# A new order of steps at the head of a fused attention and expert kernel, and two routing steps one product sooner

## The chip, the cores and the metric

The kernel runs on one core of a Trainium2 chip. The metric is the time of one execution on the device in microseconds (us), lower is better; the time of a kernel is the median of its runs.

## The reference

The first half is a cross-attention between tokens and a small recurrent state; its output feeds a mixture of experts, in which each token goes to one expert, or to that of the token before it where a gate says so.

```python
# x: 8 x 8 heads x 512 tokens x 64;  state: 8 x 8 x 32 x 64
scores = x @ state.T / 8;  a = softmax(scores);   xread = a @ state      # 512 rows for each batch
scores2 = state @ x.T / 8; a2 = softmax(scores2); sread = a2 @ x         # 32 rows for each batch
x = concat([xread, sread]) with the heads side by side                   # 8 x 576 tokens x 512
logits = x @ w_gate;  local_gate = sigmoid(x @ w_local)
for b, s:                              # in order, since an expert can be the one before
    e = argmax(logits[b, s]) if s == 0 or local_gate[b, s] < 0.5 else the expert of token s - 1
    out[b, s] = softmax(logits[b, s])[e] * (relu(x[b, s] @ w1[e]) @ w2[e])
```

w1 has 8 x 512 x 1024 and w2 8 x 1024 x 512 numbers, all float32.

## The kernel before, in words

Each of the 8 batches is a *unit* of 512 tokens that are all put through one expert (that of the batch's first token); what doesn't fit is done later in small tiles. A unit's two matrix products are made by a scheme with seven products of half size in place of eight, which needs sums and differences of quarters of its operands: `first_sum` (four of w1's quarters), `column_sum` (four of the tokens' quarters), `second_sum` (of w2's). They are made on VectorE (DVE). A unit has four halves with seven products each, 28 in all; `seven` (line 985) writes their order: 1, 5, 6, 2, 7, 3, 4 in the first matrix product. Two PSUM banks take turns with a third, `sum`; product 5 of the next half can only begin when DVE has read product 3 of the half before out of its bank.

All instructions are written out in Python order, and each engine runs its own in that order; an engine waits when the next instruction's operand isn't ready. The order comes from tables. `HEAD` (line 140) is a list of steps that stand ahead of the first product of unit 0: attention for batches 0 and 1. A step is two letters and its batch (and half): `sc` scores on TensorE (PE), `tr` 32x32 transposes on DVE, `mx`, `mo` maxima, `sb` subtraction on GpSimd (POOL), `ex`, `et` exponentials on ScalarE (ACT), `zh`, `zs`, `zi` sums of the exponentials and their inverses, `ml` their shares (POOL), `tb` transposing back (DVE, tile a), `tu` and `ec` transposes on PE and their copy by ACT, `sr`, `st`, `rt` the state's reads, their scaling (ACT) and transpose (DVE, tile rt), `sl`, `lg` logits of state and token rows (PE), `lt` their transpose, `fe` the expert of the first token (five small DVE instructions, and for batch 0 the load of that expert's weights on the SP queue), `vv` the tokens' reads (PE), `xr`, `xd` their copies by ACT or DVE, `ga`, `gl` products of the gate's weights and their copy, `kp n` n matmuls on zeros.

`BESIDE` gives what batch 1 still has to do after that, each name behind the number of a *tick*: a tick is one product of the experts, counted from 1, and its steps are written behind that product. `FLOW` does the same for batches 2 to 7, with 14 ticks for a batch. `GROUPS` gives ticks for the seven parts of `Routing.choose`, which works out each token's expert for batches 0 and 1, 2 and 3, and 4 to 7: part 1 compares logits on DVE, part 2 is an exponential, part 3 transposes on PE (line 585), part 4 is the scan over tokens on DVE (lines 590 and 591), part 5 transposes back on PE (line 601).

In unit 0 the sums of the tokens' and weights' quarters were written where `run` begins (two each, behind HEAD) and at tick 2 (the other two each).

Of the kernel before, what the change touches and what calls it, by code (L numbers as in the profile page):

```python
# [116 lines left out]
class Slots:  # L117


    def __init__(self, pool):  # L120
# [17 lines left out]


HEAD = """  # L140
sc0 tr01 tr00 kp3 ga mo01 mo00 sb01 sc1 gl mx00 sb00 mx01 ex01 tr10 nb0 ex00 zh01 tr11 et00 zh00 zs01 mo10 et01 kp7
tu00 zs00 sb10 zi01 zi00 tu01 mo11 ec00 ml01 mx11 ex10 ec01 mx10 ml00 tb01 kp2 sr0 sb11 iv0 tb00 st0 nb1 kp1 lg0 zh10
ex11 rt0 vv0 lt0 et11 zh11 zs10 fe0 xr02 xd03 et10 sl0 zs11 tu11 xd01 xr00 zi10 zi11 tu10 sk0 ml10 ec11 iv1 ec10
ml11 tb10 kp2 sr1 tb11
"""


BESIDE = """
1 lg1 vv1 st1 / 2 xr10 xr11 lt1 / 3 rt1 fe1 sl1 / 4 xr12 xr13 sk1 / 6 wr12 wr13 / 7 wr10 wr11 / 8 ws0 / 10 ws1 /
11 wr00 wr01 / 12 wr02 wr03  # L150
"""


# [4 lines left out]
"""  # L158
FIRST, PERIOD = 2, 14
PER = 28  # L160
GROUPS = {(0, 2): (6, 9, 9, 11, 13, 14, 15), (2, 4): (57, 60, 61, 62, 64, 65, 67),
          (4, 8): (103, 105, 106, 107, 110, 111, 112)}
ONES = 18, 19, 21, 22, 24, 25, 27, 28, 29

# [1 line left out]
class Attention:  # L166
# [74 lines left out]
    def do(self, name, *at):  # L241
        steps = dict(xt=self.load_t, xn=self.load_n, sc=self.scores, mx=self.maximum, nb=self.scaled, tr=self.turned,
                     zh=self.halves, mo=self.over_states, sb=self.subtract, ex=self.exponents, zs=self.sums,
                     zi=self.inverses, ml=self.shares, tb=self.turn_back, et=self.exponents_over_tokens, tu=self.turn,
                     ec=self.turned_to, iv=self.invert, sr=self.state_reads, st=self.states_to, rt=self.states_turned,
                     ws=self.states_to_rows, sl=self.state_logits, sk=self.state_logits_kept, lg=self.logits,
                     lt=self.logits_turned, vv=self.token_reads, xr=self.reads_kept, xd=self.reads_kept_too,
                     wr=self.reads_out, ga=self.gates, gl=self.gates_kept, kp=self.keep, fe=self.first_expert)
        steps[name](*at)

    def flow(self, at):

        for part in BESIDE.split("/"):
            tick, *names = part.split()
            for name in names:
                at(int(tick), self.named, name)
        for part in FLOW.split("/"):
            tick, *names = part.split()
            for b in range(2, B):
                for name in names:  # L260
                    at(max(3, FIRST + PERIOD * (b - 2) + int(tick)), self.named, name, b)
        for b in range(3, B):
            for h in range(2):
                at(FIRST + PERIOD * (b - 3) + 1, self.load_t, b, h)
            at(FIRST + PERIOD * (b - 3) + 16, self.load_n, b)
        return FIRST + PERIOD * (B - 3) + 32
# [204 lines left out]
class Routing:  # L471
# [82 lines left out]
    def choose(self, bank, b0, b1):  # L554
# [34 lines left out]
        hold, run = self.hold[:n], self.ran[:n]  # L589
        nc.vector.tensor_scalar(hold, seq, 0.0, None, Alu.is_equal)  # L590
        nc.vector.tensor_tensor_scan(run, hold, seq, 0.0, Alu.mult, Alu.add)
        zp = flat(self.zp)
        nc.vector.tensor_reduce(zp, pr, axis=AX, op=Alu.add)
# [210 lines left out]
class Experts:  # L804
# [72 lines left out]
    def at(self, tick, do, *args):  # L877
        self.todo.setdefault(tick, []).append(lambda: do(*args))

    def tick(self):  # L880
        self.ticks += 1
        for do in self.todo.pop(self.ticks, ()):
            do()
# [5 lines left out]
    def run(self, start):  # L889
# [13 lines left out]
        h11, h21, c12, h22 = [fh.tile([P, FK // 2, UNIT // 2], F32, name=f"h{i}") for i in range(4)]  # L903
        h1 = ctx.enter_context(tc.tile_pool(name="h1", bufs=1))
        ending = ExitStack()
        for i in range(2):
            self.column_sum(i)
            self.first_sum(i)

        tile_at = {}  # L910

# [260 lines left out]
        at = self.at  # L1172
# [4 lines left out]
                    at(PER * u + 18 + i, self.column_sum, i)  # L1177
                    at(PER * u + 22 + i, self.first_sum, i)
        start.flow(at)
        for do, i in ((self.column_sum, 2), (self.first_sum, 2), (self.first_sum, 3), (self.column_sum, 3)):  # L1180
            at(2, do, i)
        at(2, start.zero_row)
        for (b0, b1), ticks in GROUPS.items():
            self.steps(route.choose(start.bank, b0, b1), *ticks)
        tick = max(max(t) for t in GROUPS.values()) + 1
        at(tick, tiles_begin)
# [100 lines left out]
```

## Time and profile before

| | |
|---|---|
| median of 3 runs | 503.4 us (502.07, 504.11, 503.40) |
| the profiled execution | 505.37 us, of which the trace's span is 503.6 us |
| PE busy | 486.3 us, 97% of the span |
| DVE busy | 271.3 us, 54% |
| ACT busy | 161.2 us, 32% |
| POOL busy | 73.8 us, 15% |
| chain that ended last | PE 90%, DVE 3%, DMA 3% |
| mean granted clock of PE | 0.991 of 2.4 GHz |

An engine's busy time is the union of its instructions' spans. A row of the timeline gives an instruction's start, its length and, in brackets, how long the engine stood idle before it and what ended that. The span leaves out 1.8 us of the execution that lie around it.

### The profile page before, as it was taken

The numbers are of one execution on the slowest core, as the hardware profiler recorded it, in microseconds if no ns is written. First come the engines' busy times: TensorE is split into PE (matmuls) and PEld (weight loads), VectorE is DVE, ScalarE is ACT, GpSimd is POOL, SyncE is SP. The second block draws the span as 40 slices with busy tenths as digits, with TensorE's granted clock in tenths as the row PEclk, the third lists the DMA queues.
The fourth block names the chain that finished last, engine by engine and source line by source line (L and its number), as shares of the span: only waits on it lengthen the run. The fifth ranks groups of instructions, "written<-read, shape, count | busy, mean of one in ns | idle before, by whom it ended". The sixth has DMA issues, their size and how long they took to land.

```text
span 503.6 us, 9993 instructions
## 1 busy us (share of the span) xinstructions
PE 486.3 (97%) x4008; PEld 392.2 (78%) x4008; DVE 271.3 (54%) x540; ACT 161.2 (32%) x334; POOL 73.8 (15%) x100
## 2 busy tenths in 40 slices
PE   8779999999999899999999999999999999999994
PEld 2447788787878678888888888888888888888883
DVE  5867885585955858436475945155241632535211
ACT  2524325345343353434222322222123221223210
POOL 6601132212221122200000020000101000000000
PEclk9998999999999899999999999999999999999999
DMA  8966382845929148261717986693998659694411
GB/s 313 343 268 224 130 328 68 271 174 182 367 105 313 49 162 306 89 211 42 286 49 255 402 320 215 241 381 123 401 378 323 241 210 405 229 352 163 169 50 48
DMA packets 40479, 115.66 MB, mean 230 GB/s; under 512 B 7764, under 2 KB 8152, under 8 KB 36200
## 3 DMA queue, kind: packets, MB, share of 16 engines
q1 hardware_dynamic: 39704, 113.76, 61.7%
q0 software_dynamic: 576, 1.12, 0.6%
q8 instruction: 33, 0.54, 0.4%
q14 instruction: 22, 0.18, 0.1%
q10 hardware_dynamic: 144, 0.07, 0.0%
HBM read 97.10 MB, written 17.89 MB: 228 GB/s over the span
## 4 chain that ended last, share of the span: by engine, by line
PE 90%; DVE 3%; DMA 3%; POOL 1%; SPq 1%; issue 1%; ACT 0%; DVEq 0%; POOLq 0%
PE ps L1102 23%; PE ps L1056 21%; PE sum L1102 16%; PE sum L1056 16%; PE ps L972 3%; PE ps L959 3%; PE s L320 2%; DMA a<-in_w_dram 1%; DMA x_t<-in_xt_dram 1%; PE p L390 1%; PE p L403 1%; PE s L449 1%; DVE a L848 1%; PE p L435 1%; POOL e L380 0%
## 5 line engine op out<-in xcount | busy, mean ns | idle before, releaser
L1056 PE MATMUL ps<-x,a 128*128 128x256 f32 x384 | 92.9, 385 | 1.5 <-DMA a<-in_w_dram 1.5
L1056 PE MATMUL sum<-xs,a 128*128 128x256 f32 x384 | 92.8, 385 | 0.0
L1056 PEld LDWEIGHTS ps<-x,a 128*128 128x128 f32 x384 | 72.2, 192 | 17.2 <-issue 5.8
L1056 PEld LDWEIGHTS sum<-xs,a 128*128 128x128 f32 x384 | 73.4, 193 | 10.9 <-issue 0.6
L1102 PE MATMUL ps<-c,h 128*128 128x256 f32 x264 | 63.4, 383 | 0.0
L1102 PE MATMUL ps<-c,hs 128*128 128x256 f32 x256 | 60.7, 380 | 0.0
L1102 PE MATMUL sum<-c,h 128*128 128x256 f32 x248 | 58.6, 379 | 0.0
L1102 PEld LDWEIGHTS ps<-c,h 128*128 128x128 f32 x264 | 49.1, 190 | 11.1 <-issue 5.0
L1102 PEld LDWEIGHTS ps<-c,hs 128*128 128x128 f32 x256 | 48.5, 190 | 6.6
L1102 PEld LDWEIGHTS sum<-c,h 128*128 128x128 f32 x248 | 47.1, 190 | 6.4
L848 DVE TENSOR_TENSOR a<-a,a 128x1024 f32<-128x1024 f32 x32 | 39.6, 1275 | 5.5 <-DMA a<-in_w_dram 5.3
L848 DVE TENSOR_TENSOR c<-c,c 128x1024 f32<-128x1024 f32 x32 | 38.9, 1249 | 1.8 <-DMA c<-in_w_dram 1.5
L848 DVE TENSOR_TENSOR h<-s,s 128x512 f32<-128x512 f32 x16 | 11.1, 692 | 52.2 <-ACT s L1085 52.1
L992 ACT COPY sum<-ps 128x512 f32<-128x512 f32 (+1 forms) x32 | 14.8, 464 | 55.9 <-PE ps L1056 29.0
L1056 PE MATMUL ps<-xs,a 128*128 128x256 f32 x128 | 30.9, 384 | 1.2 <-DVE a L848 1.2
L1085 ACT COPY s<-sum 128x512 f32<-128x512 f32 x32 | 18.8, 586 | 39.4 <-PE sum L1056 39.1
L848 DVE TENSOR_TENSOR xs<-x 128x512 f32<-128x512 f32 x16 | 10.9, 679 | 38.1 <-DMA x<-xts 38.1
L1102 PE MATMUL sum<-c,hs 128*128 128x256 f32 x128 | 30.7, 382 | 0.0
L924 POOL DMA_INDIRECT xgt<-rows,state x9 | 10.0, 1111 | 139.7 <-DMA ct<-in_w_dram 74.7
L1106 ACT ACTIVATE s<-sum,prob 128x256 f32<-128x256 f32 x32 | 15.2, 474 | 43.6 <-PE sum L1102 43.6
L1056 PEld LDWEIGHTS ps<-xs,a 128*128 128x128 f32 x128 | 24.3, 191 | 5.3 <-DVE a L848 2.1
L848 DVE TENSOR_TENSOR y<-s,s 128x256 f32<-128x256 f32 x16 | 6.7, 421 | 37.9 <-ACT s L1106 37.8
(187 smaller groups left out, 560.3 us busy)
## 6 DMA issues: line engine op xcount, KB each, us to landing
at<-in_w_dram SPq DMA_DIRECT2D x18, 1024.0 KB, 6.7
ct<-in_w_dram SPq DMA_DIRECT2D x18, 1024.0 KB, 8.0
a<-in_w_dram SPq DMA_DIRECT2D x32, 512.0 KB, 7.4
c<-in_w_dram SPq DMA_DIRECT2D x32, 512.0 KB, 9.1
x_t<-in_xt_dram SPq DMA_DIRECT2D x16, 512.0 KB, 4.6
x_n<-in_xn_dram SPq DMA_DIRECT2D x8, 1024.0 KB, 12.2
out_dram<-y SPq DMA_DIRECT2D x31, 256.0 KB, 4.1
xts<-xr SPq DMA_DIRECT2D x28, 256.0 KB, 2.6
```

Source lines behind the costliest of these rows:

```text
L320: self.nc.tensor.matmul(s[u][32 * k:32 * k + 32, :], lhsT=self.states(b)[r, k, :], rhs=self.get(f"x_t{k // 2}", b)[r, k % 2, :], start=Tru ...
L390: self.nc.tensor.transpose(t[:, q], self.get("e2", b, u)[:, q], self.route.ident)
L403: self.nc.tensor.matmul(r[32 * k:32 * k + 32, u, :], lhsT=e[:, c, u, 32 * k:32 * k + 32], rhs=x_n[:, c, u, k, :], start=(c == 0), stop=(c ...
L848: self.nc.vector.tensor_tensor(out, a, b, op=op)
L924: nc.gpsimd.indirect_dma_start(out=to.rearrange("p k x -> p (k x)"), out_offset=None, in_=rows.rearrange("n q x -> (n q) x"), in_offset=ba ...
L959: nc.tensor.matmul(hps[SQ * g:SQ * g + SQ, :], lhsT=self.x_t[:, j, :], rhs=a[:, j, :, g], start=(j == 0), stop=(j == KT - 1))
L972: nc.tensor.matmul(yps[SQ * g:SQ * g + SQ, :], lhsT=self.h[:, m, :], rhs=self.ct[:, 2 * m // FK, g // 2, m % (FK // 2), g % 2 * P:g % 2 * ...
L992: nc.scalar.copy(y, x)
L1056: nc.tensor.matmul(to[:, m * width:m * width + width], lhsT=w[:, j, f:f + P], rhs=x[:, j, :], start=begin and m == 0 and j == 0, stop=(m = ...
L1085: return lambda t: nc.scalar.copy(to, t)
L1102: nc.tensor.matmul(to, lhsT=x[:, m, n * P:n * P + P], rhs=w[:, m, :], start=begin and m == 0, stop=(m == FK // 2 - 1), skip_group_check=True)
L1106: return lambda t: nc.scalar.activation(to, t, Act.Copy, scale=p)
```

## The change

The tables HEAD and BESIDE get another order, the four column sums and four weight sums of unit 0 become steps with names (`cs`, `fs`) that stand in these tables, as does the write of a zero row (`ze`), and in GROUPS three numbers are one lower: parts 1 and 2 for batches 0 and 1 (6 to 5, 9 to 8) and part 4, the scan, for batches 2 and 3 (62 to 61). FLOW's steps for batch 2 begin at tick 4 in place of 3. No instruction is added or removed.

```diff
 HEAD = """
-sc0 tr01 tr00 kp3 ga mo01 mo00 sb01 sc1 gl mx00 sb00 mx01 ex01 tr10 nb0 ex00 zh01 tr11 et00 zh00 zs01 mo10 et01 kp7
...
+sc0 kp1 tr01 kp2 tr00 mo01 sc1 mo00 sb01 mx01 kp3 sb00 mx11 ex01 kp7 tr11 zh01 ex00 mx00 ga zs01 zh00 mx10 nb0 zi01
...
 BESIDE = """
-1 lg1 vv1 st1 / 2 xr10 xr11 lt1 / 3 rt1 fe1 sl1 / 4 xr12 xr13 sk1 / 6 wr12 wr13 / 7 wr10 wr11 / 8 ws0 / 10 ws1 /
...
+1 lg1 lt1 cs3 fe1 fs3 fs2 xr12 / 2 ze / 3 xr11 / 4 sl1 sk1 / 6 wr12 wr13 / 7 wr10 wr11 / 8 ws0 / 10 ws1 / 11 wr00 wr01 /
...
-GROUPS = {(0, 2): (6, 9, 9, 11, 13, 14, 15), (2, 4): (57, 60, 61, 62, 64, 65, 67),
+GROUPS = {(0, 2): (5, 8, 9, 11, 13, 14, 15), (2, 4): (57, 60, 61, 61, 64, 65, 67),
           (4, 8): (103, 105, 106, 107, 110, 111, 112)}
...
-                at(max(3, FIRST + PERIOD * (b - 2) + int(tick)), self.named, name, b)
+                at(max(4, FIRST + PERIOD * (b - 2) + int(tick)), self.named, name, b)
...
-        for i in range(2):
-            self.column_sum(i)
-            self.first_sum(i)
...
-        for do, i in ((self.column_sum, 2), (self.first_sum, 2), (self.first_sum, 3), (self.column_sum, 3)):
-            at(2, do, i)
-        at(2, start.zero_row)
```

Three places show what moves. The first is DVE about the first sums of unit 0; a_92 to a_95 are the weights' quarters, a_96 to a_98 their sums (a_94 is written over by the third), xs the tokens' sums, and rt batch 1's transposed state reads. Before:

```order
L384 STREAM_TRANSPOSE a<-e_372 128x512
L848 TENSOR_TENSOR xs_88<-x 128x512
L848 TENSOR_TENSOR a_96<-a_94,a_95 128x1024
L848 TENSOR_TENSOR xs_89<-x,xs_88 128x512
L848 TENSOR_TENSOR a_97<-a_96,a_92 128x1024
L439 STREAM_TRANSPOSE lt<-p 128x128
L848 TENSOR_TENSOR xs_90<-x 128x512
L848 TENSOR_TENSOR a_94<-a_92,a_94 128x1024
L848 TENSOR_TENSOR a_98<-a_93,a_97 128x1024
L848 TENSOR_TENSOR xs_91<-x,xs_89 128x512
L413 STREAM_TRANSPOSE rt<-ys 128x128
```

And now:

```order
L385 STREAM_TRANSPOSE a<-e_392 128x512
L849 TENSOR_TENSOR xs_90<-x 128x512
L414 STREAM_TRANSPOSE rt<-ys 128x128
L849 TENSOR_TENSOR xs_89<-x,xs_88 128x512
L849 TENSOR_TENSOR a_96<-a_94,a_95 128x1024
L849 TENSOR_TENSOR a_97<-a_96,a_92 128x1024
L440 STREAM_TRANSPOSE lt<-p 128x128
L849 TENSOR_TENSOR xs_91<-x,xs_89 128x512
```

The transpose of rt and three of the four token sums now stand ahead of the first sum of weights; behind these rows come the five small instructions of the first expert and then a_98 and a_94.

The second is PE in the same stretch; a product on x or xs and a is one of the experts' products, L423 and L424 are the state's logits of batch 1, L320 and L321 the scores of batch 2, L449 and L450 the token reads of batch 1, of which the last of 16 matmuls stands here. Before:

```order
L449 MATMUL p<-a,states_of 32x512 x2
L1056 MATMUL ps<-xs_88,a_96 128x256 x4
L1056 MATMUL sum<-xs_89,a_97 128x256 x4
L423 MATMUL p<-wgs,rt 32x9 x4
L320 MATMUL s<-x_t_161,sttc_143 32x512 x4
L320 MATMUL s<-x_t_163,sttc_143 32x512 x4
L1056 MATMUL ps<-x,a_93 128x256 x4
L1056 MATMUL sum<-xs_90,a_94 128x256 x4
```

And now:

```order
L450 MATMUL p<-a,states_of 32x512 x2
L1054 MATMUL ps<-x,a_92 128x256 x4
L436 MATMUL p<-a,gl 32x128 x8
L1054 MATMUL ps<-xs_88,a_96 128x256 x4
L1054 MATMUL sum<-xs_89,a_97 128x256 x4
L1054 MATMUL ps<-x,a_93 128x256 x4
L424 MATMUL p<-wgs,rt 32x9 x4
L321 MATMUL s<-x_t_161,sttc_143 32x512 x4
L321 MATMUL s<-x_t_163,sttc_143 32x512 x4
L1054 MATMUL sum<-xs_90,a_94 128x256 x4
```

The token reads have moved from behind product 1 (on a_92) to ahead of it, and product 2 (on a_93) from behind the state's logits and the scores to ahead of them.

The third is DVE in unit 2, at the scan for batches 2 and 3; h and hs are the hidden rows of a half and their sums, of which the second h reads product 3 out of its bank. Before:

```order
L848 TENSOR_TENSOR hs_613<-hs_612,h_615 128x512
L1079 SCALAR_TENSOR_TENSOR h_617<-h_617,h_615 128x512
L350 TENSOR_REDUCE m_1635<-e_1748 128x16
L590 TENSOR_SCALAR hold<-p 2x544
L591 SCALAR_TENSOR_TENSOR ran<-hold,p 2x544
L593 TENSOR_REDUCE zp<-pr 128x10
L594 TENSOR_SCALAR zp<-zp 128x10
L595 RECIPROCAL zp<-zp 128x10
L848 TENSOR_TENSOR hs_614<-h_616,hs_613 128x512
```

And now:

```order
L591 TENSOR_SCALAR hold<-p 2x544
L592 SCALAR_TENSOR_TENSOR ran<-hold,p 2x544
L594 TENSOR_REDUCE zp<-pr 128x10
L595 TENSOR_SCALAR zp<-zp 128x10
L596 RECIPROCAL zp<-zp 128x10
L849 TENSOR_TENSOR h_652<-s_1655,s_1653 128x512
L849 TENSOR_TENSOR h_651<-ps,s_1654 128x512
L1075 SCALAR_TENSOR_TENSOR hs_646<-h_651,h_652 128x512
L849 TENSOR_TENSOR hs_647<-hs_646,h_649 128x512
```

The scan (named SCALAR_TENSOR_TENSOR here, line 592) and what goes with it stand ahead of the half's sums in place of behind them. In unit 0, part 1 of the routing for batches 0 and 1 (lines 571 to 577) has moved in the same way, from behind the five sums of the first half to ahead of them.

## Rows read from the trace of the kernel before

**Rows 1.** The page: the span.
```profile
span 503.6 us, 9993 instructions
```
**Rows 2.** Waits of PE: engine line <- what ended it: us in total, times, longest.
```profile
PE p L423 <- DVE first L546: 2.0, 1, 2.0
PE p L601 <- DVE ran L591: 1.7, 1, 1.7
```
**Rows 3.** Timeline of PE, 24 to 45 us: start, length, line, tiles, [idle before].
```profile
25.25 1.99 PE L1056 MATMUL ps<-x,a 128*128 128x256 f32 x8 [1.50 <-DMA a<-in_w_dram]
27.17 0.64 PE L435 MATMUL p<-a,gl 128*32 128x128 f32 x16
...
30.70 1.99 PE L1056 MATMUL ps<-xs,a 128*128 128x256 f32 x8 [1.17 <-DVE a L848]
32.53 1.90 PE L1056 MATMUL sum<-xs,a 128*128 128x256 f32 x8
36.42 0.39 PE L423 MATMUL p<-wgs,rt 128*32 128x9 f32 x8 [1.99 <-DVE first L546]
36.74 1.87 PE L320 MATMUL s<-x_t,sttc 64*32 64x512 f32 x16
38.54 2.86 PE L1056 MATMUL ps<-x,a 128*128 128x256 f32 x8
41.24 1.89 PE L1056 MATMUL sum<-xs,a 128*128 128x256 f32 x8
```
**Rows 4.** Windows: length, busy of PE, PEld, DVE, ACT, POOL, then granted clock, DMA.
```profile
37.00:40.00 3.00, 3.00 (x20) 1.19 (x5) 1.35 (x5) 0.00 (x0) 0.00 (x0) 0.50 0.11 35
...
170.00:173.00 3.00, 3.00 (x9) 2.38 (x8) 2.93 (x7) 0.59 (x1) 0.00 (x0) 0.51 0.00 0
```
**Rows 5.** Timeline of DVE, 19 to 38 us.
```profile
19.08 0.44 DVE L371 TENSOR_REDUCE z<-zh 128x16 f32<-128x272 f32 x1
...
20.16 0.14 DVE L552 CAST first<-first 1x1 int32<-1x1 f32 x1
...
24.23 0.71 DVE L384 STREAM_TRANSPOSE a<-e 128x512 f32<-128x512 f32 x1 [0.29 <-POOL e L380]
...
29.42 1.23 DVE L848 TENSOR_TENSOR a<-a,a 128x1024 f32<-128x1024 f32 x1 [3.90 <-DMA a<-in_w_dram]
...
33.10 2.35 DVE L848 TENSOR_TENSOR a<-a,a 128x1024 f32<-128x1024 f32 x2
...
35.96 0.31 DVE L413 STREAM_TRANSPOSE rt<-ys 128x128 f32<-128x128 f32 x1
```
**Rows 6.** Timeline of PE, 57 to 66 us: the scores of batch 3.
```profile
60.81 1.09 PE L320 MATMUL s<-x_t,sttc 64*32 64x512 f32 x16
```
**Rows 7.** Timeline of PE, 156 to 176 us.
```profile
167.99 0.25 PE L601 MATMUL p<-identb,ran 2*128 2x2 bf16 x4 [1.70 <-DVE ran L591]
...
168.58 2.40 PE L1056 MATMUL ps<-xs,a 128*128 128x256 f32 x8
170.78 3.21 PE L1056 MATMUL sum<-xs,a 128*128 128x256 f32 x8
```
**Rows 8.** Timeline of DVE, 156 to 176 us.
```profile
161.16 0.69 DVE L848 TENSOR_TENSOR h<-s,s 128x512 f32<-128x512 f32 x1 [2.86 <-ACT s L1085]
...
166.21 0.42 DVE L590 TENSOR_SCALAR hold<-p 2x544 bf16<-2x544 bf16 x1
...
168.44 0.63 DVE L848 TENSOR_TENSOR hs<-h,hs 128x512 f32<-128x512 f32 x1
```
**Rows 9.** Timeline of DVE, 42 to 66 us.
```profile
43.78 0.69 DVE L848 TENSOR_TENSOR h<-s,s 128x512 f32<-128x512 f32 x1 [1.96 <-ACT s L1085]
...
48.49 1.03 DVE L572 TENSOR_TENSOR eq<-lt,mx 128x80 f32<-128x80 f32 x1
...
50.35 0.68 DVE L848 TENSOR_TENSOR hs<-h,hs 128x512 f32<-128x512 f32 x1
```
**Rows 10.** Timeline of POOL, 42 to 66 us.
```profile
48.38 1.05 POOL L357 TENSOR_TENSOR e<-e,m 128x512 f32<-128x512 f32 x1 [5.43 <-DVE m L350]
```

More of the change, by code (lines that the diff above doesn't have):

```diff
@@ L140 @@
 HEAD = """
-sc0 tr01 tr00 kp3 ga mo01 mo00 sb01 sc1 gl mx00 sb00 mx01 ex01 tr10 nb0 ex00 zh01 tr11 et00 zh00 zs01 mo10 et01 kp7
-tu00 zs00 sb10 zi01 zi00 tu01 mo11 ec00 ml01 mx11 ex10 ec01 mx10 ml00 tb01 kp2 sr0 sb11 iv0 tb00 st0 nb1 kp1 lg0 zh10
-ex11 rt0 vv0 lt0 et11 zh11 zs10 fe0 xr02 xd03 et10 sl0 zs11 tu11 xd01 xr00 zi10 zi11 tu10 sk0 ml10 ec11 iv1 ec10
-ml11 tb10 kp2 sr1 tb11
+sc0 kp1 tr01 kp2 tr00 mo01 sc1 mo00 sb01 mx01 kp3 sb00 mx11 ex01 kp7 tr11 zh01 ex00 mx00 ga zs01 zh00 mx10 nb0 zi01
+et01 zs00 ml01 tr10 et00 tu01 zi00 mo10 nb1 ml00 gl tb01 ec01 sb10 tu00 tb00 et10 mo11 lg0 ec00 sb11 lt0 et11 vv0 fe0
+ex10 iv1 sr0 ex11 iv0 xd03 xr02 zh11 xr00 xd01 tu10 zh10 st0 zs11 tu11 zi11 ec10 cs0 ml11 zs10 ec11 zi10 rt0 sr1 ml10
+tb11 sl0 st1 kp2 sk0 tb10 cs2 vv1 rt1 cs1 xr10 xr13 fs0 fs1
 """
 BESIDE = """
-1 lg1 vv1 st1 / 2 xr10 xr11 lt1 / 3 rt1 fe1 sl1 / 4 xr12 xr13 sk1 / 6 wr12 wr13 / 7 wr10 wr11 / 8 ws0 / 10 ws1 /
-11 wr00 wr01 / 12 wr02 wr03
+1 lg1 lt1 cs3 fe1 fs3 fs2 xr12 / 2 ze / 3 xr11 / 4 sl1 sk1 / 6 wr12 wr13 / 7 wr10 wr11 / 8 ws0 / 10 ws1 / 11 wr00 wr01 /
+12 wr02 wr03
 """
@@ L247, in do @@
                      lt=self.logits_turned, vv=self.token_reads, xr=self.reads_kept, xd=self.reads_kept_too,
-                     wr=self.reads_out, ga=self.gates, gl=self.gates_kept, kp=self.keep, fe=self.first_expert)
+                     wr=self.reads_out, ga=self.gates, gl=self.gates_kept, kp=self.keep, fe=self.first_expert,
+                     cs=self.work.column_sum, fs=self.work.first_sum, ze=self.zero_row)
         steps[name](*at)
```

## The prediction

> **What bounds the kernel now.** Read first the page's busy times: PE is busy in nearly all of the span of 503.6 us [rows 1], and most of the chain that ended last is PE. So only time in which PE stands idle, or runs at its lower clock, can be won by an order of steps. Next, the list of PE's waits: its two longest, 2.0 and 1.7 us, are both for DVE [rows 2]. Then the timeline of PE, to see where they lie. The first is ahead of the state's logits of batch 1 (line 423): product 6 begins at 32.53, and the logits begin only at 36.42, after 1.99 us of idling [rows 3]. The reason is on DVE: the transpose of rt, which the logits read, is the last of a string of sums that DVE starts at 29.42, when the weights land, and it ends at 35.96 + 0.31 = 36.27 [rows 5]. Nothing in rt needs the weights; it only stands behind them. Product 2, which needs no sum at all, stands on PE behind the logits. The second long wait is ahead of line 601 at 167.99, for the scan of batches 2 and 3, which DVE starts at 166.21 behind five sums and a maximum [rows 7, 8].
>
> Last, the windows with the granted clock: after each of these two idles comes a stretch at half of 2.4 GHz, 0.50 in 37 to 40 us and 0.51 in 170 to 173 [rows 4]. The shorter idles of 1.50 and 1.17 ahead of products 1 and 5 were not followed by one: products 5 and 6 took 1.99 and 1.90, where product 2 in the half-clock stretch took 2.86 [rows 3]. What such a stretch costs is read from pairs: at the head, scores of 1.87 against 1.09 for the same 16 matmuls later [rows 3, 6], and product 2 of 2.86 against 1.99, 0.78 + 0.87 = 1.65. In unit 2, products of 2.40 and 3.21 [rows 7] against 1.99 and 1.90 [rows 3], 0.41 + 1.31 = 1.72.
>
> **The change part by part.** The sum is made against the profiled execution of 505.37 us.
>
> *Weights of unit 0.* Between the transpose of the logits and the expert of batch 0 DVE no longer has the 0.44 us sum at 19.08 [rows 5]. The load, and with it all of products 1, 5 and 6, comes about 0.4 earlier. Bounds: 0, if other DVE work of the new order is ahead of it, and 0.8, as on POOL the shares of batch 0 no longer stand behind a subtraction of batch 1 (1.05 for that shape [rows 10]). I take 0.4, the row nearest to it: product 5 then begins at 30.70 - 0.4 = 30.3.
>
> *The wait for rt.* DVE idles 3.90 us ahead of its first weight sum [rows 5], in which rt (0.31) and two token sums fit; they cost nothing there. On PE product 2 follows product 6 at once and the logits find rt ready. Gain 1.99. What is late next is product 7, for the sum a_94, which now stands behind a_98, a token sum and the five steps of the first expert. From 29.0 DVE has two weight sums (2.4, twice 1.2 by 29.42's row), a small transpose (0.31, as rt's), one token sum (0.7), five small steps (0.9 at most: 19.52 to 20.30) and two weight sums of 2.35 [rows 5]: 35.7. PE comes to product 7 at 30.3 + three products of 1.83 (the pitch from 30.70 to 32.53) + 0.3 for the logits + 1.0 for the scores = 37.1 [rows 3, 6]. So 1.4 to spare, and the gain stays whole; bounds 0 and 1.99.
>
> *Token reads ahead of product 1.* Before, logits and reads of batch 1 filled PE from 27.17 to 29.53 (30.70 less the idle of 1.17), 2.36 us, between products 1 and 5 [rows 3]. Now the logits alone (0.64) stand there, and product 5 still waits for the weights. Reads can start once a is turned back, 24.23 + 0.71 = 24.94 [rows 5], and take at most 2.36 - 0.64 = 1.7; so product 1 begins between 24.9 (25.25 - 0.4) and 26.6, logits end 1.92 + 0.64 later, at 27.5 to 29.2, and PE idles 1.1 to 2.8 ahead of product 5. I take 1.8. This idle costs nothing by itself, as the weights set product 5. But it is as long as the two that were followed by half clock, so I count the head's stretch as moved to products 5, 6 and 2, not as gone: gain 0, bounds 0 and 1.65.
>
> The Trainium skill, "TensorE: Matmul & The Clock Gate", section "HAM oscillation — how this bites in real kernels", blames idle gaps of PE longer than any of these for the fall of its clock. The trace differs: 0.50 and 0.51 followed idles of 1.99 and 1.70 [rows 4, 7]. By the page's rule the 1.8 would not lower the clock either; that is the first rival.
>
> *The scan of batches 2 and 3.* Its tick 61 is the one behind which PE has transposed its input. DVE has idled 2.86 us there ahead of a sum at 161.16 [rows 8], so the scan and what goes with it, 168.44 - 166.21 = 2.23 us, fill that idle's end and push the half's sums to about 163.4; the second of them, which frees product 3's bank, ends by 164.8 (two of 0.69). PE wants that bank at 167.99 - 1.70 = 166.3 [rows 7]. So 1.5 to spare, and the wait of 1.70 goes, with it the half-clock stretch: 1.70 + 1.72 = 3.42. Bounds: 1.70, if the clock falls for another reason, and 3.42.
>
> *Part 1 of the routing for batches 0 and 1*, ahead of the first half's sums. It takes 50.35 - 48.49 = 1.86 and some 0.25 for the maximum ahead, 2.1, where DVE idled 1.96 (41.82 to 43.78) [rows 9]. That idle began 5.08 after the scores began at 36.74 and will begin 4.3 after them without the half clock (5.08 - 0.78). Scores now begin at 36.1, DVE is free at 40.4, part 1 ends at 42.5 and the second sum at 43.9. PE wants the bank four products of 1.8 behind the scores' end at 37.1, at 44.3 (44.0 at a pitch of 1.73). I cost it at 0.2; bounds 0, the spare just worked out, and 2.1, all of part 1.
>
> The Trainium skill, "SBUF — State Buffer", section "SBUF: two separate sides", says that a DVE instruction with two SBUF inputs and a POOL instruction that reads SBUF exclude each other. The trace agrees: the comparison of 1.03 at 48.49 ends at 49.52, just behind the end of POOL's subtraction at 48.38 + 1.05 = 49.43 [rows 9, 10]. As POOL's first subtraction of batch 2 waits for the maximum that DVE makes right ahead of part 1, they will meet again, by that page; if they didn't, part 1 would be some 0.8 shorter, and the 0.2 would be 0.
>
> *All else* (matmuls on zeros, gate products later, the zero row, copies of batch 1's reads by ACT) moves on engines that are idle more than half of the time, or in the head's shade of the weights; 0, and if the cover is gone, some tenths through the weights' load, held in its bounds.
>
> Sum: 505.37 - 0.4 - 1.99 - 0 - 3.42 + 0.2 = 499.8. The median of the runs shown is 503.4, 2.0 under the profiled execution, and the four times spread over 3.3 us, two such half-clock stretches. I read this as stretches that don't come in every execution. After the change one can come where two could, so its median should lie less far under 499.8: half a stretch, 0.8. The forecast is 499.0.
>
> **The rivals.**
>
> *The clock stays up after the new idle.* By the rule above, or because 1.8 turns out shorter: 499.8 - 1.65 = 498.1. For: idles of 1.50 and 1.17 did nothing. Against: 1.70 did. Chance 0.20.
>
> *The head gains nothing, the wait moves.* DVE becomes late for product 7 by as much as it was for rt: 505.37 - 0.4 - 3.42 = 501.6, or about 500.8 in the median by the same 0.8. For: DVE now makes expert and token sums ahead of a_94. Against: 1.4 to spare. Chance 0.12; below and above 500.9 evenly.
>
> *Routing ahead of the units' own sums stalls PE, and the kernel is slower.* One mechanism, in unit 0 and again in unit 2: DVE takes routing first, the sum that frees product 3's bank comes late, PE idles up to 2.1 and 2.23 and falls to half clock behind each, 1.7 each: 499.8 + 4.33 + 3.4 = 507.5. It decides where that sum ends later than product 1 of the next half; I work out 0.1 to 0.4 to spare in unit 0 and 1.5 in unit 2. For: the first spare is thin. Against: the stall is what exceeds the spare, not all of the routing. Chance 0.05.
>
> **How the numbers follow.** Forecast 0.55 (its own range 498.4 to 500.6), clock stays up 0.20, head gains nothing 0.12, slower 0.05; the 0.08 that is left is for half-clock stretches that come and go otherwise, around 501 to 503. The range: at the low end 498.1 with the bounds of 0.8 for the weights and no cost of part 1, 497.5, less 0.6 for the spread of runs: 496.9. At the high end the head's gain lost, 501.6. Faster or slower means by over 0.5%, about 2.5 us, what a measurement of this kernel can tell: under 500.9 or over 505.9. Faster: 0.55 + 0.20 + 0.06 = 0.81, less 0.02 for the forecast's upper end, 0.79; slower 0.05; the same 0.16.
>
> **What would show it.** Right: no wait ahead of the state's logits of batch 1 and none ahead of line 601's successor in unit 2; product 2 directly behind product 6; PE from product 5's start to product 7's in about 7 us in place of 10.5 (30.70 to 41.24), or under 9 with half clock; the clock at full level after 166 us; an idle of 1.1 to 2.8 ahead of product 5. Wrong: a new wait for a sum ahead of product 7, or of product 5 of the second half; the load of the first weights no earlier than 21 us; a clock of 0.5 anywhere behind the head.

## The result, and the profile after

The changed kernel takes 498.9 us (median of 4 runs, 498.75 to 499.5) against 503.6 for the kernel before in the same comparison: a ratio of 0.9914, 95% interval 0.9891 to 0.9937. Timed again later it took 498.6 (6 runs), ratio 0.9917 (0.9889 to 0.9944). The profiled execution took 498.75 us.

The page's line on the span of the changed kernel, 6.6 us under [rows 1]:

```profile
span 497.0 us, 9994 instructions
```

Its list of PE's waits (us in total, times, longest), against [rows 2]: the two long waits, for the state's logits and the scan, are gone, and what stands at the top lies in the head, ahead of the first weights.

```profile
PE p L436 <- DVE a L385: 1.7, 1, 1.7
PE p L284 <- DVE warm L219: 1.2, 1, 1.2
PE s L450 <- DVE a L385: 1.1, 1, 1.1
PE s L321 <- DMA x_t<-in_xt_dram: 0.7, 1, 0.7
PE ps L1054 <- DVE a L849: 0.6, 1, 0.6
```

PE in the head, as in [rows 3] (start, length, line, tiles, idle before):

```profile
17.84 1.08 PE L436 MATMUL p<-a,gl 128*32 128x128 f32 x16 [1.74 <-DVE a L385]
...
27.77 1.99 PE L1054 MATMUL ps<-x,a 128*128 128x256 f32 x8
29.70 0.64 PE L436 MATMUL p<-a,gl 128*32 128x128 f32 x16
30.98 1.99 PE L1054 MATMUL ps<-xs,a 128*128 128x256 f32 x8 [0.64 <-DVE a L849]
32.81 1.89 PE L1054 MATMUL sum<-xs,a 128*128 128x256 f32 x8
34.54 1.89 PE L1054 MATMUL ps<-x,a 128*128 128x256 f32 x8
36.36 0.42 PE L424 MATMUL p<-wgs,rt 128*32 128x9 f32 x8
36.71 1.09 PE L321 MATMUL s<-x_t,sttc 64*32 64x512 f32 x16
37.73 1.99 PE L1054 MATMUL sum<-xs,a 128*128 128x256 f32 x8
```

Product 2 (34.54) follows product 6 at once, the logits (36.36) wait for nothing, and the scores take 1.09 where they took 1.87. From product 5 to product 7 it is 6.75 us, where it was 10.54.

The windows with the granted clock, as in [rows 4] (length; busy of PE, PEld, DVE, ACT, POOL; clock; DMA): the two stretches at 0.50 are gone, and one has come at 17 to 20 us, with the 1.74 us of idling ahead of batch 0's logits (before, PE idled 0.65 there).

```profile
17.00:20.00 3.00, 2.16 (x39) 1.11 (x48) 2.15 (x7) 2.19 (x5) 2.00 (x2) 0.55 1.05 429
37.00:40.00 3.00, 3.00 (x27) 2.01 (x12) 2.08 (x4) 0.30 (x2) 0.10 (x1) 1.00 0.28 93
...
170.00:173.00 3.00, 3.00 (x15) 2.65 (x14) 1.17 (x4) 2.00 (x4) 1.38 (x2) 1.00 0.00 0
```

In unit 2, answering [rows 7, 8], the scan is on DVE at 157.65, ahead of the half's sums; PE's transposes of its result start at 162.46 without a wait. Three lines of DVE and two of PE:

```profile
157.65 1.27 DVE L592 TENSOR_TENSOR_SCAN ran<-hold,p 2x544 bf16<-2x544 bf16 x1
...
159.43 0.63 DVE L849 TENSOR_TENSOR h<-s,s 128x512 f32<-128x512 f32 x1
159.97 0.68 DVE L849 TENSOR_TENSOR h<-ps,s 128x512 f32<-128x512 f32 x1
```

```profile
162.46 0.25 PE L602 MATMUL p<-identb,ran 2*128 2x2 bf16 x4
...
163.05 1.99 PE L1054 MATMUL ps<-xs,a 128*128 128x256 f32 x8
```

Where the time went is read by taking each product's start in the one trace from its start in the other. Product 5 of unit 0 is 0.29 us later; product 2 is 4.00 earlier; from the second half of unit 0 all products are 3.77 earlier; behind unit 2's scan all are 6.6 earlier, to the end. So the head gave 3.77 and unit 2 gave 2.83, and nothing else moved.

### The profile page after: what moved, and what is told of

It reads as the page before. It is cut to its first block, busy times and chain, and to the rows that moved or that the text cites. A ratio compares the mean times of both kernels' runs of the same rounds, so it can differ in the third digit from the quotient of the medians.

```text
span 497.0 us, 9994 instructions
## 1 busy us (share of the span) xinstructions
PE 484.2 (97%) x4006; PEld 391.5 (79%) x4008; DVE 273.4 (55%) x540; ACT 160.8 (32%) x334; POOL 76.7 (15%) x100
## 4 chain that ended last, share of the span: by engine, by line
PE 93%; DMA 3%; DVE 1%; SPq 1%; POOL 0%; issue 0%; DVEq 0%; POOLq 0%
PE ps L1100 23%; PE ps L1054 22%; PE sum L1054 17%; PE sum L1100 16%; PE ps L970 3%; PE ps L957 3%; PE s L321 1%; DMA x_t<-in_xt_dram 1%; DMA a<-in_w_dram 1%; PE p L404 1%; PE p L391 1%; PE s L450 1%; PE p L436 1%; POOL e L381 0%; DVE nb L329 0%; SPq L839 0%
## 5 line engine op out<-in xcount | busy, mean ns | idle before, releaser
L1054 PE MATMUL sum<-xs,a 128*128 128x256 f32 x384 | 91.5, 381 | 0.0
L1054 PEld LDWEIGHTS sum<-xs,a 128*128 128x128 f32 x384 | 72.3, 190 | 11.1 <-issue 1.4
L849 DVE TENSOR_TENSOR c<-c,c 128x1024 f32<-128x1024 f32 x32 | 40.4, 1296 | 1.5 <-DMA c<-in_w_dram 1.3
L849 DVE TENSOR_TENSOR h<-s,s 128x512 f32<-128x512 f32 x16 | 11.0, 687 | 44.0 <-ACT s L1083 43.9
L358 POOL TENSOR_TENSOR e<-e,m 128x512 f32<-128x512 f32 x16 | 19.0, 1188 | 53.4 <-DVE m L351 53.4
```

Of the source, the lines that this page charges most:

```text
L358: self.nc.gpsimd.tensor_tensor(e1, e1, self.each("m1", b, u), op=Alu.subtract)
L849: self.nc.vector.tensor_tensor(out, a, b, op=op)
L1054: nc.tensor.matmul(to[:, m * width:m * width + width], lhsT=w[:, j, f:f + P], rhs=x[:, j, :], start=begin and m == 0 and j == 0, stop=(m = ...
```

## The experiments

Nine more kernels were timed, one of them twice, and the changed kernel again. In "before + ..." the kernel before has only the edit shown, and lines of an edit can be cut (...); times are medians, and a ratio is to the kernel before in the same comparison.

**The scan alone.** Before + one number:

```diff
-GROUPS = {(0, 2): (6, 9, 9, 11, 13, 14, 15), (2, 4): (57, 60, 61, 62, 64, 65, 67),
+GROUPS = {(0, 2): (6, 9, 9, 11, 13, 14, 15), (2, 4): (57, 60, 61, 61, 64, 65, 67),
```

> The kernel before with one number changed: part 4 of the routing (the scan) for batches 2 and 3 at tick 61 in place of 62. Theory (PE's two long waits for DVE and the half-clock stretch behind each carry the gain): the wait of 1.70 us ahead of line 601 at 168 us goes, and the half-clock stretch at 170 us (1.72) with it, so 2.8 (what unit 2 gave in the changed kernel) to 3.4 us in the profiled span; the head stays as it is. Rival (the head's new order makes the whole gain): no change, within 0.3 us.

Measured: 502.3, ratio 0.998 (0.9964 to 0.9997). In its trace unit 2 is 2.83 us shorter, to the hundredth what the whole change gave there, and the head is as before, its half clock included. PE's transposes of the scan's result and the head's window:

```profile
165.94 0.25 PE L601 MATMUL p<-identb,ran 2*128 2x2 bf16 x4
```

```profile
37.00:40.00 3.00, 3.00 (x22) 1.92 (x7) 2.22 (x5) 0.00 (x0) 0.18 (x1) 0.54 0.39 119
```

The median moved only 1.1: unit 2's half clock, which the profiled execution of before had, is not in every execution (below).

**The head alone.** The changed kernel with the ticks of GROUPS as they were:

```diff
-GROUPS = {(0, 2): (5, 8, 9, 11, 13, 14, 15), (2, 4): (57, 60, 61, 61, 64, 65, 67),
+GROUPS = {(0, 2): (6, 9, 9, 11, 13, 14, 15), (2, 4): (57, 60, 61, 62, 64, 65, 67),
```

> The changed kernel with the three numbers of GROUPS as before: only the head's order. Theory: PE waits 1.70 us ahead of line 601 in unit 2 again, with a half-clock stretch behind it; the head keeps its 3.4 to 3.8 us against the kernel before. Rival (head makes the whole gain): 6.5 us less than the kernel before in the profiled span, no wait in unit 2.

Measured: 501.8, ratio 0.9971 (0.995 to 0.9992). Its head gives 2.81 us, less than the 3.4 to 3.8 expected: product 5 comes 0.80 later than before (last section), and part 1's gain (below) is not in it. Its unit 2 gives nothing: the idle of 1.70 and the half clock behind it are there. But the 1.74 us idle in its head was *not* followed by half clock (window 17 to 20 us at 1.00), while the same idle of the changed kernel was, in both its traces:

```profile
17.00:20.00 3.00, 1.74 (x39) 0.67 (x47) 2.38 (x8) 2.20 (x6) 2.19 (x3) 1.00 1.04 426
...
167.00:170.00 3.00, 3.00 (x9) 2.38 (x8) 2.93 (x7) 0.59 (x1) 0.00 (x0) 0.50 0.00 0
```

**The wait for rt taken away on DVE.** Before + `st1` and `rt1` moved to the end of HEAD:

```diff
-ml11 tb10 kp2 sr1 tb11
+ml11 tb10 kp2 sr1 tb11 st1 rt1
...
-1 lg1 vv1 st1 / 2 xr10 xr11 lt1 / 3 rt1 fe1 sl1 / ...
+1 lg1 vv1 / 2 xr10 xr11 lt1 / 3 fe1 sl1 / ...
```

> The kernel before with two steps moved: scaling and transpose of batch 1's state reads (st1, rt1) stand at the end of HEAD, ahead of the first sums. PE's order is unchanged. Theory: the wait of 1.99 us ahead of the state's logits goes (they follow product 6 directly), and the half-clock stretch behind it; product 7 comes 2.0 us sooner, 3.6 if the clock stays up; a few tenths may be lost ahead of product 5. Rival (product 2 ahead of the logits on PE is what counts): less than 0.5 us at product 7.

**The wait filled on PE.** Before + the logits and the scores of batch 2 one product later:

```diff
-... / 3 rt1 fe1 sl1 / 4 xr12 xr13 sk1 / ...
+... / 3 rt1 fe1 / 4 sl1 xr12 xr13 sk1 / ...
...
-                    at(max(3, FIRST + PERIOD * (b - 2) + int(tick)), self.named, name, b)
+                    at(max(4, FIRST + PERIOD * (b - 2) + int(tick)), self.named, name, b)
```

> The kernel before with PE's order alone changed: state logits of batch 1 and scores of batch 2 one product later (ticks 4 in place of 3), so product 2 follows product 6; DVE still makes rt behind the sums. Theory (PE idles because something it needs stands behind the sums, whichever order mends it): product 2 fills the wait, rt is ready at 36.3 when the logits come, the wait and the half-clock stretch go: product 7 about 3.4 us sooner, and 1.7 without the clock. Rival (DVE's order is what counts): the wait of 2.0 stays, only behind product 2.

Measured: 500.6, ratio 0.9962 (0.9945 to 0.998), and 500.9, ratio 0.9967 (0.9949 to 0.9985). Either edit takes the wait; their heads give 3.70 and 3.42. In both traces unit 2's idle of 1.70 is untouched, and yet unit 2 is 1.68 us shorter than in the profiled execution of before, as no half clock followed. The rivals expected of the two edits, that only PE's order counts or only DVE's, are both out: either order mends it. PE and the windows of the first of them:

```profile
30.40 2.00 PE L1056 MATMUL ps<-xs,a 128*128 128x256 f32 x8 [1.85 <-DVE a L848]
...
164.30 0.25 PE L601 MATMUL p<-identb,ran 2*128 2x2 bf16 x4 [1.70 <-DVE ran L591]
```

```profile
30.00:33.00 3.00, 2.60 (x12) 2.16 (x13) 3.00 (x6) 0.57 (x2) 0.00 (x0) 1.00 1.01 374
165.00:168.00 3.00, 3.00 (x14) 2.66 (x15) 2.97 (x6) 0.59 (x1) 0.00 (x0) 1.00 0.00 0
```

So what was open: does half clock follow from these idles at all, and how often?

**Both idles filled, the waits left.** Before + 7 matmuls on zeros ahead of the logits and 7 ahead of line 601:

```diff
-... / 3 rt1 fe1 sl1 / ...
+... / 3 rt1 fe1 kp7 sl1 / ...
...
+        at(64, start.keep, 7)
         for (b0, b1), ticks in GROUPS.items():
```

> The kernel before with 7 matmuls on zeros put into each of the two idle times (ahead of the batch 1 logits in the head, and ahead of the counts' matmul in unit 2), the waits themselves left as they are. Theory 1 (the idle time of 1.7 to 2.0 us is what half clock follows, in some runs): no run shows the lower granted clock, all runs at 0.996 to 0.997, median 501.4, which is where the undisturbed runs of the kernel before lie, 2.0 below its median of 503.4; no group at 503.5 or 505. Theory 2 (half clock comes at these places whatever TensorE does there): three groups of runs as before, median 503 to 503.5.

Measured: 501.8 over 12 runs, 501.24 to 502.31, ratio 0.9978 (0.996 to 0.9995). The kernel before had, over its 68 runs beside these experiments, three groups: 25 runs at 500.7 to 502.7 (median 501.7, granted clock 0.996 or 0.997 in 21), 34 at 502.9 to 503.9 (503.5, 0.993 or 0.994 in 32), 9 at 504.7 to 505.2 (504.9, 0.990 or 0.991). With the fill only the first group is left; two of its 12 runs show a clock of 0.994 and 0.995 where 0.996 was expected. The mean clock is a rough sign: it also counts the last 2 to 5 us of the span, which are at half clock in every trace, and the profiled run with the fill has 0.995 and no other stretch. The waits still end when they did, and PE does useless work in them. PE at the two places, and the windows behind them:

```profile
34.34 1.67 PE L283 MATMUL p<-zero 128*128 128x512 bf16 x7
36.49 0.39 PE L423 MATMUL p<-wgs,rt 128*32 128x9 f32 x8 [0.48 <-DVE first L546]
...
164.56 1.67 PE L283 MATMUL p<-zero 128*128 128x512 bf16 x7
166.42 0.25 PE L601 MATMUL p<-identb,ran 2*128 2x2 bf16 x4 [0.19 <-DVE ran L591]
```

```profile
37.00:40.00 3.00, 3.00 (x26) 1.94 (x11) 2.09 (x6) 0.14 (x1) 0.00 (x0) 1.00 0.33 101
167.00:170.00 3.00, 3.00 (x15) 2.65 (x15) 2.96 (x4) 0.59 (x1) 0.00 (x0) 1.00 0.00 0
```

The first theory holds by the times. Against the profiled execution of before the head is 1.64 us shorter from product 5 on and unit 2 1.69: the price of a stretch, and of nothing else, since the waits stayed.

**Part 1 alone.** Before + (0, 2)'s first two ticks 5 and 8 in place of 6 and 9:

> The kernel before with (0, 2)'s first two parts alone one product sooner. Theory 1 (as predicted, this part costs 0.2 us by VectorE's order ahead of product 7 of the head): 503.5. Theory 2 (it takes away the wait of 0.3 us that TensorE has for the choice of (0, 2), which the trace of before shows, and costs nothing): 0.3 us less on the aligned starts of the products behind it, 503.0; either way three groups of runs, since both idle times stay.

Measured: 502.4, ratio 0.9987 (0.9966 to 1.0008), which can't be told from no change. In the trace the second theory is right: PE's wait of 0.3 for part 1's result (line 585), which the first line shows of the kernel before, is gone, and products behind it are 0.37 earlier. Its trace also has both long idles with the full clock behind them:

```profile
PE p L585 <- DVE top L576: 0.3, 1, 0.3
```

```profile
36.61 0.39 PE L423 MATMUL p<-wgs,rt 128*32 128x9 f32 x8 [1.99 <-DVE first L546]
36.93 1.09 PE L320 MATMUL s<-x_t,sttc 64*32 64x512 f32 x16
...
166.17 0.25 PE L601 MATMUL p<-identb,ran 2*128 2x2 bf16 x4 [1.70 <-DVE ran L591]
```

```profile
168.00:171.00 3.00, 3.00 (x32) 2.50 (x46) 2.93 (x7) 1.03 (x2) 0.00 (x0) 1.00 0.00 0
```

**Three small edits in place of the new order.** Before + `st1 rt1` at the end of HEAD + the three ticks of GROUPS, the head's order otherwise as it was:

> The kernel before with three small edits alone: the step that turns batch 1's logits moved to the end of the head, (2, 4)'s scan one product sooner, (0, 2)'s first two parts one product sooner; the head's order stays as it was before. Theory 1 (the whole gain of the change is the two waits, of 1.99 us in the head and of 1.70 us in unit 2, with the half clock that follows them in some runs): median 498.6 (498.2 to 499.1), no slower than the changed kernel; product 5 starts about 0.5 us earlier than in it, since the weights are issued without its long second issue. Theory 2 (the new order of the head carries part of the gain, by the sums and copies that it spreads): 499.5 to 500.5, with waits ahead of products 6 to 8 or of the first routing.

> The kernel with the three small edits once more, as the measure of the other in this call: 498.3 (498.0 to 498.8), every run at a granted clock of 0.995 or more.

Measured: 498.3 (498.05 to 498.76), ratio 0.9911 (0.9885 to 0.9937), and again 498.4, ratio 0.99 (0.9875 to 0.9926). The first theory holds: these edits give all that the change gave. The granted clocks were 0.995 and more as expected, but for one run of 0.991, which was the fastest (497.16). Product 5 came only 0.1 to 0.4 earlier than in the changed kernel, not 0.5. Ahead of it PE idled 1.74 in the first of the two traces and 1.72 in the second, and the clock stayed up behind it in both. The first:

```profile
30.90 1.99 PE L1056 MATMUL ps<-xs,a 128*128 128x256 f32 x8 [1.74 <-DVE a L848]
```

```profile
31.00:34.00 3.00, 3.00 (x14) 2.51 (x15) 3.00 (x5) 1.07 (x3) 0.00 (x0) 1.00 1.00 403
```

**The idle in the head of the changed kernel.** The changed kernel timed again, and with 6 matmuls on zeros ahead of batch 0's logits (`mo11 kp6 lg0` for `mo11 lg0`):

> The changed kernel itself once more, so that the others of this call can be set against it. In its first trace TensorE had one stretch of half clock, at 17.3 to 20.7 us, where TensorE waits for unit 0's weights afterwards in any case. Theory 1 (that stretch is covered by the loads of the weights): runs with a granted clock of 0.993 to 0.995 and runs with 0.996 to 0.997 take the same time within 0.5 us, median 498.9. Theory 2 (it costs its own length as in the kernel before, where the groups of runs lie about 1.9 us apart): runs of the higher clock are 1.5 to 2 us shorter than those of the lower, and the median moves with the share of each, between 497 and 499.

> The changed kernel with 6 matmuls on zeros ahead of batch 0's logits in the head, where TensorE stood idle for 1.74 us before its one stretch of half clock. Theory 1 (that stretch is covered): the stretch at 17 to 21 us goes, the routing of the first expert ends 0.4 us earlier (20.2 to 19.8 on the trace), product 5 starts 0 to 0.4 earlier, median 498.4 to 498.9. Theory 2 (it costs its length): median 497.2.

Measured: 498.6 (497.58 to 498.98) with granted clocks of 0.991 to 0.997 that the times do not follow, and 498.7 (498.12 to 499.2) with 0.996 to 0.998 in every run. So the stretch at 17 to 21 us is real, comes in most runs by their clocks, and costs nothing that can be measured. Theory 1's detail was wrong: product 5 started at 31.18, not earlier. The first load was issued 0.1 to 0.25 us earlier than in the changed kernel's two traces, and a longer second issue took that back (last section).

**One more step.** The three edits, and parts 5 and 6 for (2, 4) one product sooner as well:

```diff
-... (2, 4): (57, 60, 61, 61, 64, 65, 67),
+... (2, 4): (57, 60, 61, 61, 63, 64, 67),
```

> The three small edits of the kernel with the head of before, and (2, 4)'s parts 5 and 6 (the counts' matmul on TensorE and the copies of its results on VectorE) one product sooner as well. In the changed kernel TensorE's token reads of that place stop for 0.44 us at 167.15 us, and the trace names nobody for it; VectorE then has the copies of the counts, 167.14 to 167.62, behind two sums of unit 2's second weights that took 3.10 us together. Theory 1 (the reads wait for the bank that these copies still read): with the copies between the two sums the pause goes, and the time is 0.4 to 0.6 us below the same kernel with three edits, 497.8. Theory 2 (the pause is another wait): the pause stays, the same time within 0.2 us.

Measured: 497.7 (497.27 to 498.02), ratio 0.9889 (0.9864 to 0.9913); the kernel with three edits took 498.4 beside it. Unit 2 now gives 3.46 in place of 2.83. In the changed kernel, PE's reads stopped for 0.44 and went on at 167.59, about when DVE's last copy of the counts was done, 167.48 + 0.14 = 167.62 (PE, then DVE):

```profile
167.14 0.62 PE L450 MATMUL s<-a,states_of 32*32 32x512 f32 x2
167.15 0.61 PE L450 MATMUL p<-a,states_of 32*32 32x512 f32 x1
167.59 0.59 PE L450 MATMUL s<-a,states_of 32*32 32x512 f32 x2
```

```profile
164.12 3.10 DVE L849 TENSOR_TENSOR c<-c,c 128x1024 f32<-128x1024 f32 x2
167.14 0.16 DVE L607 CAST ex<-p 128x8 f32<-128x8 bf16 x1
...
167.48 0.14 DVE L611 SCALAR_TENSOR_TENSOR undone<-ex,p 128x8 f32<-128x8 f32 x1
```

With the copies between the two sums they end at 166.03, before the reads begin at 166.80, and the reads run through:

```profile
165.55 0.15 DVE L606 CAST ex<-p 128x8 f32<-128x8 bf16 x1
...
165.89 0.14 DVE L610 SCALAR_TENSOR_TENSOR undone<-ex,p 128x8 f32<-128x8 f32 x1
```

The pause went with the copies, as theory 1 said; that the bank is what the reads waited for is argued from the meeting of the times, since the trace names nobody. This is the fastest kernel of the study.

The copies came late also because the two sums ahead of them took 3.10, where two took 2.44 in the kernel before. The first of the two took 1.84, with a subtraction of POOL beside it (163.46 to 164.88); before, no POOL instruction ran beside them, and the first took 1.18. At 2.44 the copies would have ended at about 166.96 (an estimate), ahead of the reads at 167.14. That POOL held the sum up was not tried. The sums before, and POOL in the changed kernel:

```profile
169.21 2.44 DVE L848 TENSOR_TENSOR c<-c,c 128x1024 f32<-128x1024 f32 x2
```

```profile
163.46 1.42 POOL L358 TENSOR_TENSOR e<-e,m 128x512 f32<-128x512 f32 x1 [9.49 <-DVE m L351]
```

## Why the prediction was right

The time (499.0 against 498.9) was right, and the two waits were the right places. Of the six terms one was right and five were off, and that they came out so near is luck:

| term | predicted | measured |
|---|---|---|
| wait for rt | -1.99 | -1.99, no wait took its place |
| half clock in the head | 0 | -1.65 |
| weights of unit 0 | -0.4 | +0.29 |
| scan of (2, 4) | -3.42 | -2.83 |
| part 1 for (0, 2) | +0.2 | -0.37 |
| the median against the profiled execution | -0.8 | +0.1 |

The first five measured terms add up to 6.55, and 505.37 - 6.6 = 498.8 is the profiled execution after. Starts of products give the first two together, 3.69; the stretch is priced by the prediction's pairs of rows, and by the fill at 1.64. The forecast's terms made 499.8 of the same execution, 1.0 too much, and the 0.8 that it then took off for the median wasn't there: the four runs have 498.87, the profiled one 498.75. These two errors cancel.

*A step that failed* is "I count the head's stretch as moved to products 5, 6 and 2, not as gone: gain 0". Three things were wrong in it. The new idle ahead of product 5 was 0.64, not 1.8 (in the three other traces of the new order 0.23, 1.18 and 1.43): the reads could start only when a was turned back, which in the new order ended at 26.54 and not at 24.94, so product 1 began at 27.77 and its work reached up to the weights. An idle of that length does not bring half clock each time. In the eleven traces of the two kernels and of the experiments without a fill, PE idled 1.70 to 1.99 us between matmuls fifteen times, and never longer behind the head's first matmul; six of the fifteen were followed by half clock, and no other stretch of half clock came but in the last few us of a span. Four of the fifteen (1.72 to 1.85) lay ahead of product 5, the place that the prediction named, and none of these four was followed by one. And the stretch that did come lay at 17 us, with an idle ahead of batch 0's logits that the prediction has no term for; there PE has to wait for the weights afterwards, and the fill of it saved nothing.

So rival 1, by which the clock stays up, came true for the head, at the price it gave (1.65). The forecast had taken the stretch for something that comes in some executions only, and that part of it is now shown, by the three groups and by the fill that leaves one. What it made of that was wrong: it took half a stretch off for the changed kernel, as if one that costs could still come there. By the groups, the median run of before (503.5) had one stretch; its profiled execution had two, and the changed kernel none that costs. From median to median the change is 4.7: the waits and what went against them, 1.99 + 0.37 + 1.70 - 0.56 - 0.29 = 3.2, and one stretch of 1.65 to 1.69, makes 4.9.

*Scan.* Wait and stretch went, 1.70 + 1.69 by the fill; 0.56 of it was lost, by the pause of the reads nearly 5 us later, which the prediction didn't see. It asked what the earlier scan delays (1.5 to spare, and there was no wait), but not what the rest of the queue, now without its pauses, runs into: DVE reached the counts behind two sums of weights, one of them made longer beside POOL, and PE, which no longer waited ahead of line 601's successor, reached its reads sooner.

*Part 1.* DVE was free at 40.99 (forecast 40.4), the second sum ended at 44.32 (43.9), and PE wanted the bank at 44.74 (44.0 to 44.3): no stall, but 0.4 to spare. The forecast left out a gain that stood in the list of waits: PE's own wait of 0.3 for part 1's result. The Trainium skill's rule in "SBUF — State Buffer", section "SBUF: two separate sides", on which the 0.2 rested, held: the comparison again ended just behind POOL's subtraction (42.22 behind 42.13), and the one for batches 4 to 7, of twice the columns and with no POOL instruction beside it, took 0.33 (at 243.61).

```profile
41.19 1.03 DVE L573 TENSOR_TENSOR eq<-lt,mx 128x80 f32<-128x80 f32 x1
```

```profile
41.08 1.05 POOL L358 TENSOR_TENSOR e<-e,m 128x512 f32<-128x512 f32 x1 [0.97 <-DVE m L351]
```

*Weights of unit 0.* From the start of batch 0's logits to the expert's number it takes 2.1 us in the new order at full clock (head alone: 18.02 to 20.13) and 2.3 to 2.4 in the old. So part of the 0.4 is there, but the logits themselves start no earlier (17.84 with half clock behind them, 17.96 before), and the loads lose more: below.

## What to carry to other kernels

Before a difference against one profiled execution is summed up, look how the runs spread: where their times lie in groups with different granted clocks, the profiled one may hold a stretch of half clock that the median run lacks. An idle of PE of 1.7 to 2 us is then priced as itself and a share of such a stretch (here six of fifteen had one); where it can't be removed, matmuls on zeros in it kept the clock up here, in all of 12 runs by their times. And a new order found for a whole queue is worth undoing step by step: here three edits of single steps gave all of it, and a look at the next pause gave 0.7 us more.

## What the runs showed of the hardware

*The same idle, with and without half clock.* The identical idle of 1.70 ahead of the scan's transposes was followed by half clock in two traces and not in three; that of 1.99 in the head in two and not in one. What decides was not found; filled, none of 12 runs had it by its time.

*One issue of a load took 1.0 to 1.4 us, in the new order of the head and not in the old.* SP issues the four quarters of unit 0's first weights one after another. In all nine traces with the old order each issue took 0.33 to 0.35 us, and product 5 began 9.50 to 9.68 us behind the first issue. In all four with the new order the second issue took longer (1.02, 1.22, 1.36, 1.36), and product 5 began 9.81, 10.05, 10.36 and 10.65 behind the first. In these four a transfer of program code (16 KB) starts at 21.2 to 21.4 us, just ahead of that issue; where the order is the old one none starts between 20.6 and 22.6. The issue's row, and the queue's:

```profile
L839 SPq DMA_DIRECT2D a<-in_w_dram x1: 1222/1222/1222, 21.5 to 21.5; - x1
```

```profile
q8 instruction: 1, 0.02, 36.4%
```

The two come together in other places and in either order too: in the thirteen traces, behind their first 10 us, SP issued 90 loads and stores 0.2 to 0.6 us after the start of such a code transfer, and 70 of these issues took over 0.6 us; of the other 2458 issues 309 did. That the code's transfer holds the issue was not tried.
